# Preparation, attention and last stage of a fused attention and S4 kernel: narrow rows, no constant matmul ahead of the key burst, GpSimd work held back at unit borders

## The chip, the cores and the metric

One core of one Trainium2 chip. The time is device microseconds of one execution of the whole program. The profile is one execution, taken apart from the timed ones. All runs compared here are of the fast state, but for one of the 20 of e4, which is slow and left out of its ratio. The *granted clock* is the share of PE's full clock that the chip let through; in these traces it is 0.50 or 1.00 at any moment, and a mean for a stage or a run. A ratio is the mean time of one kernel's fast runs over the mean of the kernel before's fast runs of the same rounds, so it is not quite the ratio of the medians that stand beside it.

## The reference

Forward and backward of a gated mix of two blocks; thirteen outputs (the value and twelve gradients).

```python
B, S, D, H = 1, 2048, 576, 32             # head size 18; S4: L = 2048, N = 128 states
g = sigmoid((x * gate_w).sum(-1, keepdims=True))
a = attention(x, wqkv, wo)                # softmax(q k^T / sqrt(18)) v, then @ wo
b = S4(x, A, B, C, log_dt, Dskip)         # causal convolution with a kernel built from A, B, C
out = g * a + (1 - g) * b
_out, _vjp = jax.vjp(_f, ...)             # and the gradients for grad_out
```

## The kernel before

The attention works in 32 *units* (8 groups of 4 heads, times 4 query blocks of 512) of 32 *steps*. A step does two exponentials of 128x1024 on ScalarE: `PT` for the forward pass of one unit and `eb` (transposed scores) for the backward pass of the unit before. PE is fed in exactly the order below; all accumulators named accV, accQ, accK, accF share one PSUM bank, in turn. A *burst* is the run of matmuls into one of them, and its *eviction* is VectorE's reading it out. At a unit border VectorE makes `rl`, GpSimd from it `dOa`, and VectorE the sums `dl` from GpSimd's `prod`; between these GpSimd works through the *table products* of S4.

```python
NFILL = (0, 0, 1, 3)              # constant matmuls ahead of accV, accQ, accK bursts, and in accF
fill: mm(o_, lhsT=J_bf, rhs=fill_r)         # 128x128 times 128x512, a result nobody reads
for G in range(NTOT + OFF + 24):            # ... cut: what one step emits, in PE's order
    row(ps, KaT, QaT)                       # scores of the forward pass -> exp PT
    # G % 4 in (3, 0): accO += PT x Vtok
    row(ps, QaT, KaT)                       # transposed scores          -> exp eb
    row(ps, VaT, dOaT)                      # dP, then VectorE: ds = dP * PT
    # one of four: fill + accV, fill + accQ, fill + accK (key burst, 16 matmuls), accF (3 fills)
    # after accF: turn_ds, four PE transposes of a part of ds, in 7 of 8 cases
    ...                                     # evictions, products
    if G % NST not in (1, 2) or G >= NTOT:  # hold-back of GpSimd's table products
        e_emit(G)
```

A group's transposed keys are loaded as one block, and constants (zeros, ones, minus ones in the spare rows 18 to 31 of each head) are written on GpSimd's queue:

```python
nc.sync.dma_start(t_, KaT_d[g])             # 128 rows (4 heads x 32) of 4 KB
...
for t_ in rows:                             # Q, K, V
    nc.gpsimd.dma_start(t_[:, DH + 1:HP, sl], con[pt, 0:1, :].to_broadcast(...))
```

## Time and profile before

| | before |
|---|---|
| median, us (over all jobs 3161 to 3167) | 3162.5 |
| preparation, to the first forward exponential | 235.6 |
| attention, first PT to last eb exponential | 2119.3 |
| between attention and the weight gradients (mostly S4) | 603.8 |
| end, from the first weight-gradient matmul | 206.0 |

The stage marks are read off the timeline, and the same marks are used for every kernel below. The four rows sum to the profile's span of 3164.7. The prediction shows the profile's lines by stage.

### The profile page before, as it was taken

The numbers are of one execution on the slowest core, as the hardware profiler recorded it, in microseconds if no ns is written. First come the engines' busy times: TensorE is split into PE (matmuls) and PEld (weight loads), VectorE is DVE, ScalarE is ACT, GpSimd is POOL, SyncE is SP. The second block draws the span as 40 slices with busy tenths as digits, with TensorE's granted clock in tenths as the row PEclk, the third lists the DMA queues.
The fourth block names the chain that finished last, engine by engine and source line by source line (L and its number), as shares of the span: only waits on it lengthen the run. The fifth ranks groups of instructions, "written<-read, shape, count | busy, mean of one in ns | idle before, by whom it ended". The sixth has DMA issues, their size and how long they took to land. (4 is left out here: it accounts for less than half of the span.)

```text
span 3164.7 us, 70747 instructions
## 1 busy us (share of the span) xinstructions
PE 2580.8 (82%) x27165; PEld 1191.7 (38%) x27165; DVE 2460.3 (78%) x4533; ACT 2396.5 (76%) x2760; POOL 1811.8 (57%) x3387
## 2 busy tenths in 40 slices
PE   6668888888888888888888888888875787786668
PEld 2222222222233322323222322322224777776446
DVE  4244888888898888888888988888883888888634
ACT  3339999899899989999889988998845767675111
POOL 1009988988888898898898888888110000000010
PEclk9767999999899999999999988999986888888889
DMA  8865999888889988988998997897789778772895
GB/s 220 156 158 106 173 160 182 154 160 162 165 159 158 190 145 158 183 155 161 170 165 151 167 178 143 155 181 147 131 142 256 195 205 208 202 201 77 239 213 111
DMA packets 1411365, 533.55 MB, mean 169 GB/s; under 512 B 1309053, under 2 KB 1380190, under 8 KB 1401810
## 3 DMA queue, kind: packets, MB, share of 16 engines
q1 hardware_dynamic: 1380722, 463.03, 75.4%
q0 software_dynamic: 22416, 58.63, 7.5%
q10 hardware_dynamic: 7888, 7.38, 0.8%
q8 instruction: 212, 3.47, 0.4%
q14 instruction: 127, 1.04, 0.1%
HBM read 144.48 MB, written 102.83 MB: 78 GB/s over the span
## 5 line engine op out<-in xcount | busy, mean ns | idle before, releaser
L783 DVE TENSOR_TENSOR ds<-ps_P,PT 128x512 bf16<-128x512 f32 x2048 | 1316.0, 684 | 213.1 <-ACT eb L778 114.4
L773 ACT ACTIVATE PT<-ps_P 128x1024 bf16<-128x1024 f32 x1024 | 1049.5, 1027 | 164.8 <-PE ps_P L30 164.4
L778 ACT ACTIVATE eb<-ps_P 128x1024 bf16<-128x1024 f32 x1024 | 1051.8, 1027 | 32.3 <-PE ps_P L30 30.4
L552 POOL TENSOR_TENSOR et<-eG,eT 128x256 f32<-128x256 f32 x1152 | 701.0, 630 | 35.1
L30 PE MATMUL ps_P<-KaT_g,QaT_g 32*128 32x512 bf16 x2048 | 412.1, 393 | 86.7 <-ACT eb L778 86.5
L30 PE MATMUL ps_P<-dOaT,VaT_g 32*128 32x512 bf16 x2048 | 457.2, 394 | 5.9 <-DVE ds L783 4.4
L552 POOL TENSOR_TENSOR Eo<-et,et 128x256 bf16<-128x256 f32 x576 | 418.7, 727 | 43.1
L30 PE MATMUL ps_P<-QaT_g,KaT_g 32*128 32x512 bf16 x2048 | 416.5, 405 | 20.8 <-DMA Vtok_g<-VaT_d 12.6
L1074 POOL TENSOR_TENSOR SS<-m 128x96 f32<-128x96 f32 x18 | 7.9, 437 | 558.7 <-ACT m L1072 470.6
L30 PEld LDWEIGHTS <-QaT_g 32*128 32x128 bf16 x2048 | 154.4, 91 | 317.8 <-issue 316.6
L30 PE MATMUL accQ<-ds,Ktok_g 128*32 128x512 bf16 x2048 | 161.6, 391 | 105.5 <-DVE dvacc L489 67.1
L30 PE MATMUL accF<-ident_bf,J_bf 128*128 128x512 bf16 x783 | 233.8, 411 | 0.2 <-DVE dqa L504 0.2
L30 PEld LDWEIGHTS <-KaT_g 32*128 32x128 bf16 x2048 | 97.1, 91 | 341.1 <-issue 307.0
L30 PE MATMUL accO<-PT,Vtok_g 128*32 128x512 bf16 x2048 | 213.1, 402 | 0.0
L30 PEld LDWEIGHTS <-J_bf 128*128 128x128 bf16 x1103 | 91.7, 99 | 237.5 <-issue 207.4
L30 PE MATMUL accK<-dsT,Qtok_g 128*32 128x256 bf16 x4096 | 175.0, 296 | 0.0
L30 PE MATMUL accK<-ident_bf,J_bf 128*128 128x512 bf16 x256 | 103.0, 402 | 75.1 <-DVE dqa L509 59.9
L30 PE MATMUL accV<-eb,dOa 128*32 128x512 bf16 x2048 | 158.6, 387 | 2.2 <-DVE dsT L445 1.6
L930 ACT COPY E1e<-etp 128x1024 bf16<-128x1024 bf16 x144 | 135.9, 1043 | 17.8 <-PE etp L929 13.6
L30 PEld LDWEIGHTS <-Qtok_g 128*32 128x32 bf16 x4096 | 89.9, 100 | 157.8 <-issue 152.6
L30 PE MATMUL yp<-Rw,E1n 128*128 128x30 bf16 x1152 | 67.8, 232 | 87.9 <-DVE Rw L993 73.3
L30 PEld LDWEIGHTS <-E1n 128*128 128x128 bf16 x2304 | 96.7, 109 | 105.4 <-issue 104.9
(243 smaller groups left out, 3992.0 us busy)
## 6 DMA issues: line engine op xcount, KB each, us to landing
E_d<-Eo POOLq DMA_DIRECT2D x144, 256.0 KB, 3.6
E1n<-E_d SPq DMA_DIRECT2D x36, 1024.0 KB
xs<-xb_d SPq DMA_DIRECT2D x18, 1024.0 KB
T0w<-Kp_d SPq DMA_DIRECT2D x18, 1024.0 KB
Md_d<-mst SPq DMA_DIRECT2D x36, 288.0 KB
dsT<-ds SPq DMA_TRANSPOSE x512
dqkv_d<-dtk POOLq DMA_DIRECT2D x96, 72.0 KB, 3.8
skw<-Md_d SPq DMA_DIRECT2D x72, 64.0 KB
```

The costliest lines, as they stand in the source:

```text
L30: return nc.tensor.matmul(out, lhsT=lhsT, rhs=rhs, start=start, stop=stop, **kw)
L552: nc.gpsimd.tensor_tensor(out, a, b, op=op)
L773: nc.scalar.activation(U["PT"][i][:, j:j + 2, :], ps, ACT.Exp)
L778: nc.scalar.activation(e, ps, ACT.Exp)
L783: nc.vector.tensor_tensor(U["ds"][i][:, j, :], ps, U["PT"][i][:, j, :], op=A.mult)
L930: nc.scalar.copy(E_[:, 4 * q:4 * q + 4], pt_)
L1074: nc.gpsimd.tensor_tensor(o_[:, :, 0], m4[:, :, 0], m4[:, :, 3], op=A.subtract)
```

## The change

The intent: shorter constants and their stores out of the way of other transfers; a shorter loop at the key burst; no GpSimd work in the way at unit borders; fewer waits at the end. The core of the diff, cuts marked:

```diff
+    HS = DH + 2                                   # rows of K and V: 20 per head, not 32
-        QaT_d, KaT_d, VaT_d = ... [NG, P, S]
+        QKV_d = dram.tile([2 * HR + H * HP, S], BF, name="QKV_d")
...                                                # preparation
-            put_constants()                       # 20 stores on GpSimd's queue
+            for a_ in range(4):                   # 12 stores on SyncE's, before the first results
+                nc.sync.dma_start(rows[q_][:, y0:y1, sl], con[pt, q_:q_ + 1, :].to_broadcast(...))
+                xr_t = work.tile([P, TB, D], BF, tag="xr_t4", bufs=2, name="xr_t4")   # stores of four
...                                                # attention
-            NFILL = (0, 0, 1, 3)
+            NFILL = (0, 0, 0, 3)
+                def strip(k, g, c0, n):           # the next head's rows stand in as spare rows
+                    return bass.AP(tensor=QKV_d.tensor, ..., ap=[[WID[k] * S, 4], [S, HP], [1, n]])
-                    nc.sync.dma_start(t_, KaT_d[g])
+                    nc.sync.dma_start(t_, strip("K", g, 0, S))
-                    est = 0.07 + 2 * CE * n * 0.0023
+                    est = 0.21 + 2 * CE * n * 0.0018      # estimates that spread GpSimd's work
-                    for f in todo.pop(("f2", G), []):     # dl operations
-                        evs.append(f)
-                    for e_ in evs:
+                    for e_ in evs + todo.pop(("f2", G), []):
-                    if G % NST not in (1, 2) or G >= NTOT:
+                    if G % NST not in (0, 1, 2, NST - 1) or G >= NTOT:
...                                                # end
-                        nc.sync.dma_start_transpose(out=ob, in_=o_q)
+                            nc.tensor.transpose(pt_[:, c, :], o_q[:, c * P:(c + 1) * P], ident_bf)
-                nc.sync.dma_start(o12[d0:d0 + dsz, :], dgwb[0:dsz, c:c + 1])   # 576 single elements
+                nc.sync.dma_start(aps_out["out_12"]..., dgwb)                  # one row
+                    ob = work.tile([P, D], BF, tag="dwo_bf", bufs=3, name="dwo_bf")
```

## The prediction

> **What bounds the kernel now.** I read the busy time by stage first, then a steady stretch of the attention, the waits of each engine, and the queue of the preparation's transfers. By stage (columns: window, its length, busy us of PE, PE weight load, VectorE, ScalarE, GpSimd, the granted clock, the DMA share, GB/s):
>
> ```profile
> 0.00:233.50 233.50, 158.55 (x533) 60.15 (x533) 95.56 (x219) 71.61 (x121) 22.40 (x49) 0.79 0.79 179
> 277.60:2284.00 2006.40, 1733.01 (x17678) 591.49 (x17679) 1735.51 (x3068) 1844.04 (x1969) 1707.70 (x3182) 0.95 0.90 162
> ...
> 2944.70:3048.80 104.10, 65.18 (x332) 33.93 (x333) 43.99 (x66) 10.38 (x20) 12.03 (x19) 0.81 0.86 249
> 3048.80:3128.00 79.20, 79.15 (x635) 62.44 (x635) 51.49 (x95) 12.40 (x16) 0.00 (x0) 0.98 1.02 219
> ```
>
> The preparation (0 to 233.5, when the first score matmul starts) has no engine that is full: it is a chain of waits. The attention takes two thirds of the span and has four engines at 85 to 92%. The convolution (2371 to 2945) is untouched by the change and stays at 574. The end, 220 us, is PE work with three waits.
>
> A steady step of the attention, in order of start (start, duration, engine, line, operation; in brackets the idle time before it and who ended it):
>
> ```profile
> 758.71 0.68 DVE L509 SCALAR_TENSOR_TENSOR dqa<-accQ,dqa 128x512 f32<-128x512 f32 x1
> 759.44 0.38 PE L30 MATMUL accK<-ident_bf,J_bf 128*128 128x512 bf16 x1 [0.23 <-DVE dqa L509]
> ...
> 759.75 0.62 PE L30 MATMUL accK<-dsT,Qtok_g 128*32 128x256 bf16 x16
> ...
> 760.73 1.02 ACT L773 ACTIVATE PT<-ps_P 128x1024 bf16<-128x1024 f32 x1 [0.16 <-PE ps_P L30]
> ```
>
> The same ScalarE exponential stood at 753.11 one period before, so a period with one key burst is 7.62 us. It holds eight exponentials that start 0.92 apart when nothing is missing, 7.36 together. The missing 0.26 is a loop: the dqa eviction, the constant matmul into accK (0.31 from its start to the key burst's), the key burst of 16, the scores, the exponential. So here ScalarE and this loop are both bounds, ScalarE 0.26 behind.
>
> At a unit border (every 32 steps) more is lost:
>
> ```profile
> 787.07 0.26 DVE L397 RECIPROCAL rl<-accF 128x16 f32<-128x16 f32 x1 [0.32 <-PE accF L392]
> ...
> 792.06 0.45 DVE L410 TENSOR_REDUCE dl<-prod 128x16 f32<-128x288 f32 x1 [2.63 <-POOL prod L404]
> 792.63 0.68 DVE L489 TENSOR_TENSOR dvacc<-dvacc,accV 128x512 f32<-128x512 f32 x1
> ...
> 794.99 1.02 ACT L773 ACTIVATE PT<-ps_P 128x1024 bf16<-128x1024 f32 x1 [3.82 <-PE ps_P L30]
> ```
>
> GpSimd has table products in its queue when rl is ready, gets to dOa 3.5 us later, and VectorE, which works in order, stands 2.63 us at dl with the dvacc eviction behind it; PE and ScalarE then stand 3.5 and 3.8, and the granted clock is 0.50 for the next 6 us. The reciprocals rl, from 271.94 to 2292.16, are 31 units apart, 65.17 us each; 32 steps at the steady 7.62 per four would be 61.0. So a border costs 4.2 us on the mean, some none, some 7.
>
> GpSimd is the one to watch. Of its waits between 300 and 2200 only one is a wait for other engines, and its most frequent instruction is the table product:
>
> ```profile
> POOL dOa L402 <- DVE rl L397: 48.4, 14, 6.2
> ```
> ```profile
> L552 POOL TENSOR_TENSOR et<-eG,eT 128x256 f32<-128x256 f32 x1152 | 701.0, 630 | 35.1
> ```
>
> It is free only 48.4 of 1900 us. 1851.6 us over 1900/65.17 = 29.15 units are 63.5 us per unit: that is GpSimd's own pace, only 1.7 us under the present one.
>
> In the preparation, the in-order VectorE waits 28.8 us for the transposed d_a, and PE behind it 24.4 (in five waits 35.2) for the evictions that it owes. The transposes' own times show why:
>
> ```profile
> 72.02 22.64 SPq L243 DMA_TRANSPOSE d_aT<-d_a  x1
> 99.51 20.52 SPq L243 DMA_TRANSPOSE d_aT<-d_a  x1
> 183.92 4.36 SPq L243 DMA_TRANSPOSE d_aT<-d_a  x1
> 198.72 3.10 SPq L243 DMA_TRANSPOSE d_aT<-d_a  x1
> ```
>
> The same transfer takes 3 to 4 us when it is alone and 20 to 23 while GpSimd's queue stores 5.4 MB of constants (65 to 106 us). PE is idle from 88 to 112 and the granted clock is 0.50 from 80 to 120.
>
> At the end, two waits are aimed at:
>
> ```profile
> PE ps_a L30 <- DMA OT<-O_tok: 21.8, 1, 21.8
> PE ps_dwq L30 <- DMA dq_all<-dqkv_d: 16.5, 1, 16.5
> PE ps_dwo L30 <- ACT dwo_bf L1359: 8.6, 1, 8.6
> ```
>
> **What the Trainium skill says.** "TensorE: Matmul & The Clock Gate", Part 1: the clock is granted at 4/8 or 8/8 by how busy PE was in recent windows of about 3.4 us, and idle gaps above some 3 us should be avoided. The trace has only 0.50 and 1.00, in agreement, but at 782.9 it falls after 1.4 us of idle spread over 3.4, so the share counts and not only one long gap. "GPSIMD Engine Reference", 3.1: an operation with two input tensors takes about 2.6 cycles per element at 1.2 GHz, an estimate of 555 ns for 256 elements; the trace has 630, so such work has no slack to give. "DMA: Bandwidth & Descriptors", section on issuing engines not being separate queues: transfers issued by another engine share the same DMA engines. The trace agrees: GpSimd's stores slow SyncE's transposes from 3 to over 20 us. So moving the constants to SyncE does not make them cheaper; it only moves them in time. Same page, specifications: transfers below 512 B cost a read-modify-write. The small output of 576 two-byte pieces starts at 3129.00, and a store that starts 6 us after it took 15.32.
>
> **The change part by part.**
>
> *Preparation.* Constants and parameter blocks go out on SyncE's queue ahead of the first projection stores, with rows of 20 elements in place of 32 for K and V and fewer, larger blocks (12 for 30). They fall then before, not on, the d_a transposes. Gain: most of PE's 24.4 us stall, and the clock of the 40 us at 0.50: some 25 of these are busy after the stall is gone and could be run up to twice as fast, which I take as 10 us. The larger weight loads come after the first input transpose and x is loaded earlier: 7.2 + 2.7 of PE waits, I take 6. Larger stores (four tiles at once) and full 128-row operands: 3. Cost: the first projection store comes after 2.2 MB of constants, by my count of the queue at about 62 us and not 44; three staging buffers cover only part, so I charge 10 for a new stall, and 4 for the K strips that now load in four pieces. Sum: 24 + 10 + 6 + 3 + 9 - 14 = 38, where the 9 is the larger clock share in the dO part (176 to 222, where 0.83 and 0.66 are granted): less certain.
>
> *Attention, fill.* The constant matmul at the key burst goes (256 times). The loop falls from 7.62 to 7.31, below ScalarE's 7.36, so a period gains 0.26. There are 985 steps of 2.037 us here, about 246 periods, some 220 of them undisturbed: 57 us. In the tail, ten more periods, 3.
>
> *Attention, borders.* The products are held back in the last step of a unit and the first three, and the dl operations come behind the evictions. At 13 borders dl waited 27.5 us for prod; with the restart at half clock I put it at 1.5 times, 41.
>
> *The joint limit.* 57 + 41 = 98 us over 31 units would be 62.0 per unit, but GpSimd needs 63.5. Its work is not reduced, and the changed hold-back takes away places for it. So the two gains are worth together at most (65.17 - 63.5) x 31 = 52, and as no stage reaches its bound I take 0.8 of it: 42, plus 1 in the tail.
>
> *End.* Parameter gradients are turned by PE in place of six DMA transposes; but these 30 transposes stand in PE's order behind all 320 weight-gradient matmuls, so the work pool comes free nearly as late: 1. The O load waits for fewer transposes, 0 to 3. The small output becomes 32 wide matmuls and one row in place of 80 matmuls and 576 pieces, 16 x 0.15 = about 2. dwo_bf has three buffers: the 8.6 stall goes, and with it the cold run of the last 64 matmuls (10.1 against about 7.8): 11, less what the last store still takes. Sum about 11.
>
> Total: 38 + 43 + 11 = 92, from 3162.5 to 3070.
>
> **The rivals.** *(1) GpSimd is the bound at once, and unevenly:* where the held-back products pile up behind a border, every unit has slow steps, and the attention gains 15 to 20 only. For: the 63.5. Against: the new cost estimates spread its work more evenly over the units (it was up to 65.8 in some and 61.7 in others). Time 3095. *(2) The clock:* without the constant matmul PE's share falls from about 78 to 74% in the steady state; if that leaves a window under the threshold, matmuls double in time and the attention loses 50 to over 100. For: the fall at 782.9. Against: steady windows with 75% stand at 1.00, and the threshold seen lies near 58%. Time 3150 to 3250. *(3) The stall in the preparation only moves:* constants ahead of the first stores hold the staging buffers back for 15 to 20 us; gain there 10 to 20, time 3090. *(4) The preparation gains more:* with no idle gap PE stays warm through dO, 16 tiles of 3.43 us go toward 2: gain 55, time 3050. *(5) Less at the end:* the OT wait of 21.8 stays and the last store still ends the run: gain 5.
>
> **Range and chances.** The three parts are nearly independent: preparation 20 to 55, attention 20 to 57, end 5 to 25. Their spreads of about 15, 15 and 7 add in squares to 22; with a little for the clock the range is 3030 to 3112. The line of 2% is at 3100, 1.3 such spreads above 3070. So faster by over 2% has 0.80, within 2% 0.17, slower 0.03, for rival 2.
>
> **What would show it.** Right: the group accK from the constant is gone; a steady period is 7.36 to 7.5; the wait of dl for prod is below 10 in all; dOa's wait for rl shrinks from 48.4 toward 0 and units are about 63.5 apart (GpSimd the bound). The first score matmul is at about 195, the d_a transposes take 3 to 6 us each, and PE shows a new wait for staging buffers between 48 and 64. The dwo wait is gone and the OT wait is still near 20; the convolution is 574. Wrong: a granted clock in the attention below 0.93; units still 65 apart with dOa waiting (then the loop was not the bound); units under 63 (then GpSimd's pace was not one); a first score matmul after 215 or before 180.

## The result

3162.78 us median (3155.69 to 3165.82, 4 runs) against 3163.26; ratio 0.9997, interval 0.9979 to 1.0016. The time is the same. The stages are not:

| us, from the profiles | before | after | difference |
|---|---|---|---|
| preparation | 235.6 | 206.6 | -29.0 |
| attention | 2119.3 | 2153.8 | +34.5 |
| to the first weight-gradient matmul | 603.8 | 602.0 | -1.8 |
| end | 206.0 | 199.1 | -6.9 |
| span | 3164.7 | 3161.5 | -3.2 |

So two parts gained 36 us as meant, and the attention, where 43 were expected, lost 34. Stages of the kernel after (same columns as in the prediction):

```profile
0.00:204.50 204.50, 127.44 (x532) 69.90 (x532) 94.90 (x220) 70.00 (x120) 11.21 (x29) 0.84 0.79 189
...
243.00:2300.00 2057.00, 1759.86 (x17522) 599.38 (x17521) 1745.92 (x3087) 1860.41 (x1978) 1716.50 (x3196) 0.92 0.92 159
```

The granted clock of the attention is 0.92, where it was 0.95. That is the first trace of what happened.

**The steady step.** The group of the constant matmul at accK is gone, and yet the period is 7.62 us, as before. Kernel after, one period, in order of start:

```profile
961.48 0.62 PE L30 MATMUL accK<-dsT,Qtok_g 128*32 128x256 bf16 x16 [0.23 <-DVE dqa L523]
961.58 1.03 ACT L790 ACTIVATE eb<-ps_P 128x1024 bf16<-128x1024 f32 x1
...
962.67 0.39 PE L30 MATMUL ps_P<-dOaT,VaT_g 32*128 32x512 bf16 x2
...
963.12 1.29 DVE L795 TENSOR_TENSOR ds<-ps_P,PT 128x512 bf16<-128x512 f32 x2 [0.16 <-PE ps_P L30]
...
963.88 0.38 PE L458 MATMUL dst_p<-ident_bf,ds 128*128 128x128 bf16 x4
...
964.20 0.39 PE L30 MATMUL ps_P<-QaT_g,KaT_g 32*128 32x512 bf16 x2
...
964.63 1.02 ACT L785 ACTIVATE PT<-ps_P 128x1024 bf16<-128x1024 f32 x1 [0.18 <-PE ps_P L30]
```

The gap of ScalarE is no longer behind the key burst; it stands one step later, behind the four transposes of ds. The chain: `eb` must end, PE can then do the scores with dO (962.67), VectorE the first product ds (963.12), PE the transposes (963.88), which stand in PE's order *ahead* of the next scores (964.20), and those feed the exponential at 964.63. From `eb` to that `PT` it is 3.05 us, and three exponentials need only 3 x 0.92 = 2.76. The same chain is in the kernel before:

```profile
759.54 1.03 ACT L778 ACTIVATE eb<-ps_P 128x1024 bf16<-128x1024 f32 x1
...
761.84 0.38 PE L444 MATMUL dst_p<-ident_bf,ds 128*128 128x128 bf16 x4
...
762.59 1.02 ACT L773 ACTIVATE PT<-ps_P 128x1024 bf16<-128x1024 f32 x1
```

Again 3.05 us from `eb` (759.54) to `PT` (762.59). But the page gave this exponential no wait: the one before it had been delayed by the constant matmul, so ScalarE was not free before 762.57 (the eb at 761.65 and 0.92). The second loop left only some 0.02 us to gain, and the first one hid it.

**The borders.** VectorE's wait for prod is nearly gone, and GpSimd's for rl has grown (waits of the kernel after, 300 to 2200; total, times, longest):

```profile
DVE dl L424 <- POOL prod L418: 4.1, 2, 3.0
```
```profile
POOL dOa L416 <- DVE rl L411: 87.0, 24, 7.5
```

So GpSimd was not the bound: it waits 87 us here against 48. Units are 66.3 us apart (243.0 to 2298.3, 31 of them) where they were 65.17. By step within the unit, against the steady step: the first eight steps cost 3.04 us per unit, not 3.90; the other twenty-four cost 2.28, not 0.21. Two thirds of these 2.28 (8 units of 5.76 us in 30) stand in every fourth unit, where the load of a group's keys is followed, 7 to 12 us later, by stalls that cost 4.6 to 8.5 us.

**The key load.** DMA share (tenths) in 40 slices of the 17 us from the load on; after, then before:

```profile
DMA  7379324999932313231222222243999990099999
```
```profile
DMA  8699995949998990000899999903999999599259
```

After: for some 17 slices, 7 us, the engines stand at 0.1 to 0.4, and 58 to 116 GB/s flow. I read this as one transfer working on about a quarter of the engines. Before, the same 512 KB left the engines busy with other work. Behind the load stand the DMA transposes of ds; VectorE's product ds waits for them (300 to 2200; no such wait is listed before):

```profile
DVE ds L795 <- DMA dsT<-ds: 26.0, 9, 6.7
```

**The clock.** In long stretches of the attention the granted clock is 0.50 although PE never stops (kernel after, unit 16; PE busy is the second number):

```profile
1243.50:1247.00 3.50, 3.50 (x30) 0.66 (x30) 1.88 (x3) 2.89 (x3) 3.27 (x6) 0.50 0.77 114
1247.00:1250.50 3.50, 3.48 (x32) 0.94 (x33) 3.37 (x6) 2.96 (x3) 3.02 (x6) 0.50 0.25 81
1250.50:1254.00 3.50, 3.44 (x19) 1.06 (x16) 1.84 (x4) 2.18 (x3) 3.26 (x6) 0.50 0.92 181
...
1261.00:1264.50 3.50, 3.44 (x19) 1.02 (x16) 1.77 (x4) 2.25 (x3) 3.33 (x6) 0.50 1.26 155
1264.50:1268.00 3.50, 3.50 (x30) 0.70 (x30) 1.97 (x4) 2.82 (x4) 3.04 (x6) 0.50 1.25 170
```

A period takes 10.4 us there, not 7.62 (exponentials at 1250.6 and 1261.0). I counted such stretches in the clock record of each trace, from the start of unit 1 to the end of unit 30. Their lengths are multiples of 3.41 us:

| kernel | constant matmul | stretches | of 1 / 2 / 3 or more windows | longest, us | in all, us |
|---|---|---|---|---|---|
| before | yes | 35 | 21 / 12 / 2 | 17.1 | 181 |
| after | no | 35 | 14 / 8 / 13 | 30.7 | 293 |

As many stretches, but longer: 112 us more at half clock. At (10.4 - 7.62) / 10.4 = 0.27 us lost per us this is an estimate of 30 us (a fit of time against the recorded clock of each run gives 0.16 to 0.30 in the kernels timed 20 times or more). It may not be added to what the experiments below take apart, since a stall can itself be followed by half clock: putting the constant matmul back gives 6 us in the changed kernel (e1, within noise) and 13 with the key strip mended (e11 against e12).

**Preparation and end.** The stall of 24 us is gone, a new one has come. Waits of PE up to 235, and two of SyncE's issues:

```profile
PE ps L30 <- DVE sq L227: 21.1, 8, 5.5
PE psr L30 <- ACT xr_t L191: 18.1, 6, 16.5
```
```profile
52.27 10.19 SPq L172 DMA_DIRECT2D QKV_d<-con  x12
62.50 0.43 SPq L173 DMA_DIRECT2D zero_d<-con  x1
63.04 0.85 SPq L193 DMA_DIRECT2D xr_d<-xr_t  x2
...
79.68 8.00 SPq L254 DMA_TRANSPOSE d_aT<-d_a  x1
...
92.40 10.96 SPq L254 DMA_TRANSPOSE d_aT<-d_a  x1
```

The store that frees the xr_t buffers stands behind the twelve constants and goes out at 63.04; PE stands from 49.9 to 66.4. The later transposes hold SyncE's queue for 8 and 11 us in place of 20 and more. At the end the chain of waits now ends in PE work alone:

```profile
3134.13 4.01 PE pgw L30 x32
3138.14 19.84 PE ps_dwo L30 x160
```

The 8.6 us wait and the cold run are gone, and the OT wait is 9.0, not 21.8; but the new transposes and their own waits now stand in that time, and from the last weight-gradient matmul to the first output matmul it is 19.1 us where it was 22.2. Against this the small output's matmuls take 4.0 us at once, and from the first output matmul to them the loop takes 87.5 us where it took 83, at a clock of 0.93.

### The profile page after: what moved, and what is told of

It is laid out like the page before. It is cut to its first block, busy times and chain, and to the rows that moved or that the text cites. A ratio compares the mean times of both kernels' runs of the same rounds, so it can differ in the third digit from the quotient of the medians.

```text
span 3161.5 us, 70115 instructions
## 1 busy us (share of the span) xinstructions
PE 2566.7 (81%) x26891; PEld 1209.8 (38%) x26891; DVE 2461.5 (78%) x4531; ACT 2405.2 (76%) x2765; POOL 1801.6 (57%) x3371
## 3 DMA queue, kind: packets, MB, share of 16 engines
q14 instruction: 127, 1.04, 0.1%
## 5 line engine op out<-in xcount | busy, mean ns | idle before, releaser
L30 PE MATMUL ps_P<-KaT_g,QaT_g 32*128 32x512 bf16 x2048 | 420.6, 401 | 125.8 <-ACT eb L790 125.0
L30 PE MATMUL ps_P<-dOaT,VaT_g 32*128 32x512 bf16 x2048 | 491.5, 403 | 33.0 <-DVE ds L795 25.1
L30 PE MATMUL ps_P<-QaT_g,KaT_g 32*128 32x512 bf16 x2048 | 425.8, 414 | 22.2 <-DMA Vtok_g<-QKV_d 14.1
L30 PE MATMUL accF<-ident_bf,J_bf 128*128 128x512 bf16 x783 | 240.6, 420 | 0.2 <-DVE dqa L518 0.2
L30 PE MATMUL accO<-PT,Vtok_g 128*32 128x512 bf16 x2048 | 222.0, 420 | 0.0
L30 PEld LDWEIGHTS <-Qtok_g 128*32 128x32 bf16 x4096 | 114.9, 99 | 181.4 <-issue 177.7
L30 PE MATMUL accV<-eb,dOa 128*32 128x512 bf16 x2048 | 168.2, 407 | 2.1 <-DVE dsT L459 1.8
L30 PEld LDWEIGHTS <-J_bf 128*128 128x128 bf16 x847 | 67.6, 101 | 190.5 <-issue 161.4
L523 DVE SCALAR_TENSOR_TENSOR dqa<-accQ,dqa 128x512 f32<-128x512 f32 x192 | 130.4, 679 | 0.0
```

Source lines behind the costliest of these rows:

```text
L30: return nc.tensor.matmul(out, lhsT=lhsT, rhs=rhs, start=start, stop=stop, **kw)
L523: nc.vector.scalar_tensor_tensor(o_, acc, c_scale, a_, op0=A.mult, op1=A.add)
```

## The experiments

Theory A: a second loop of the same length holds the steady period. Theory G, formed after the first runs: the constant matmul's worth was the clock, and without it every stall costs more. Rivals: B, the constant matmul was the bound and its gain was lost elsewhere; C, the hold-back moves the loss; D, an engine holds the period. "Attention" is from the profile of each run, the ratio is to the kernel before (after: 0.9997).

**e1: the constant matmul back.**

```diff
-            NFILL = (0, 0, 0, 3)
+            NFILL = (0, 0, 1, 3)
```

> The changed kernel with the one constant matmul at the key burst put back, nothing else. Theory A (a second loop, as long as the one through the constant matmul, holds the period: exponential, score with dO, VectorE's product ds, the transposes of ds on PE, and behind them in PE's order the next scores): the steady period of four steps stays 7.62 us and the time stays within 10 us of the changed kernel, near 3163. Rival B (the constant matmul was the bound, as I predicted, and its 57 us were gained but lost again elsewhere): the period goes from below 7.5 to 7.62 and the time rises by 40 to 60 us, to 3205 to 3220.

3157.01 us (20 runs), 0.9985; period 7.62. Theory A holds: at the key burst it gains nothing to leave the matmul out. B is out. The attention of this run's profile is 2153.9, as in the changed kernel, so alone the matmul does not bring the loss back.

**e2: the key strip in four transfers.**

```diff
-                    nc.sync.dma_start(t_, strip("K", g, 0, S))
+                    for j in range(4):
+                        r0 = ROW0["K"] + (4 * g + j) * WID["K"]
+                        nc.sync.dma_start(t_[HP * j:HP * (j + 1), :], QKV_d[r0:r0 + HP, :])
```

> The changed kernel with each load of a group's key strip (128 rows of 4 KB, now one transfer whose slowest dimension is the 4 heads) given out as four transfers of 32 rows each. Theory A (the one transfer runs on a quarter of the DMA engines, takes some 12 us, and holds up the transposes of ds behind it once per group of four units): the stalls of 4 to 8 us in the middle of every fourth unit go, and the time falls by 25 to 45 us, to some 3120 to 3138. Rival C (the slow middle of units comes from GpSimd's held-back products that bunch up behind the border): the time stays within 10 us of 3163.

3140.95 us, 0.9938: 22 us less than the changed kernel, a little under what I gave. DMA share from the load on, 17 us:

```profile
DMA  9223999879994999999989939905999999999493
```

The quarter-full stretch is gone. Steps 8 to 31 of every fourth unit lost 5.76 us in the changed kernel and lose 2.44 here, and the wait for the transposes has fallen from 26.0 us:

```profile
DVE ds L797 <- DMA dsT<-ds: 6.4, 5, 3.3
```

The edit changes two things, the slowest dimension and the number of transfers; e5 bears on which of them counts.

**e3: the transposes of ds behind the next scores.**

```diff
-                            evs.append(turn_ds(UN[(g, b)], q_))
+                            at(("turn", G + 1), lambda U=UN[(g, b)], q_=q_: turn_ds(U, q_)())
...                    # after the scores of PT in the next step:
+                    for f in todo.pop(("turn", G), []):
+                        f()
```

> The changed kernel with the four PE transposes of ds put behind the next step's first score matmuls instead of ahead of them, nothing else. Theory A (these transposes are the loop that holds the steady period at 7.62): the period falls to 7.36 to 7.45, ScalarE's own pace, and the time falls by 20 to 50 us, less the more GpSimd's pace of 63.5 us per unit binds. Rival D (VectorE or GpSimd holds the period): 7.62 stays and the time stays within 10 us of 3163.

3124.14 us, 0.9887; period 7.50, not 7.36 to 7.45. Theory A holds, D is out as it was put: with the same work on every engine, the order alone gives 38 us. But 7.50 shows a third loop (see e8).

**e4: the border as before** (hold-back of two steps, dl operations ahead of the evictions).

```diff
+                    for f in todo.pop(("f2", G), []):       # ahead of the bursts' evictions
+                        evs.append(f)
-                    for e_ in evs + todo.pop(("f2", G), []):
+                    for e_ in evs:
-                    if G % NST not in (0, 1, 2, NST - 1) or G >= NTOT:
+                    if G % NST not in (1, 2) or G >= NTOT:
```

> The changed kernel with both parts of the border change undone: products held back only in two steps of a unit as before, and the dl operations ahead of the step's evictions as before. Theory A (the border change gained about 26 us in the first eight steps of the units; the rest of the loss is the strip): the time rises by 15 to 35 us, to 3180 to 3200, and the waits of dl for prod come back toward 27 us. Rival C (the hold-back only moves the products into later steps, and costs there what it gains): within 10 us of 3163, with the slow steps in the middle of units fewer.

3144.29 us (20 runs, 3122.59 to 3178.07, the highest of them slow), 0.9952, interval 0.9934 to 0.997. My expectation was wrong: undoing the border change gains 18 us by the medians, where I had read a gain of 26 out of the first eight steps of the units. The spread is wide, and this run's profile (3158.7) is above its median. Nor do the waits of dl for prod come back toward 27 us: they are 8.6.

**e5: rows of 32 per head again, constants where the change put them.**

```diff
-    HS = DH + 2
+    HS = HP
-                    return bass.AP(tensor=QKV_d.tensor, ..., ap=[[WID[k] * S, 4], [S, HP], [1, n]])
+                    return QKV_d[r0:r0 + P, c0:c0 + n]
```

> The changed kernel with rows of K and V again 32 per head in memory, so that every strip is one contiguous block of 128 rows; the constants grow again (K's and V's 14 spare rows hold -1 and 1, which meet only zeros or unused rows), still stored by SyncE ahead of the first projection stores. Theory A (the narrow strips, read as four pieces, cost the attention some 35 us, of which giving the key strip out in four got back 19): from the first to the last exponential the time falls from 2154 to 2115 to 2130 us, near the 2119 of the kernel before, with no mid-unit stalls; the preparation gets longer by 5 to 20 us for 3 MB more of constants. Total 3130 to 3150. Rival E (the strip costs only what the four-way split recovered): the attention stays above 2135.

3149.62 us, 0.9944; attention 2136.5, preparation 219.2 to the first exponential. The preparation is 12.6 us longer, as expected; the attention is not back at 2119 and is about what e2 gives (2139.5). So the layout costs the attention about what the four-way split gets back (rival E), and another cause is left. Here the strip is again one transfer, but of 128 rows, and the quarter-full stretch is gone too (17 us from 533, the load at 533.5); VectorE's wait for the transposes of ds is 2.9 us. So one transfer alone does not make the stretch; what e2 and e5 share is that no load of the strip has a slowest dimension of 4.

```profile
DMA  9999989989109999999988915799999999969577
```

**e6: only the hold-back as before.**

```diff
-                    if G % NST not in (0, 1, 2, NST - 1) or G >= NTOT:
+                    if G % NST not in (1, 2) or G >= NTOT:
```

> The changed kernel with the products held back in two steps of a unit as before, the dl operations left behind the evictions. Undoing both parts gave about 14 to 18 us. If the longer hold-back is what costs (GpSimd stands idle at a border, 87 us in all against 48, and catches up behind it), this alone gives 10 to 20, to 3143 to 3153. If the late dl operations cost (the dO transpose behind them starts later and PE waits for it), this gives under 5, and the other half gives it.

3145.63 us (5 runs, 3129.93 to 3172.01), 0.9944, interval 0.9903 to 0.9986. The hold-back seemed to be the part that costs; see e10 and e12. VectorE's wait for prod is 2.9 us here too, so the hold-back was not what removed it. Nor is it the late dl operations alone: with early ones e8 has 27.4 but e4 only 8.6, and e14, with late ones, has 35.3. What removed it is not settled.

**e7: e3 with the constant matmul back** (the edits of e1 and e3).

> The changed kernel with the transposes of ds behind the next scores, as in the run that gave 3124, and the constant matmul at the key burst put back. Theory A (two loops of the same 7.62 us side by side, each enough to hold the period): the period returns from 7.50 to 7.58 to 7.62 and the time rises to 3140 to 3160, so that each of the two edits alone gives nothing or little where the other loop stands. Rival F (only the transposes' loop counted, the constant matmul never did): 7.50 stays and the time is within 8 us of 3124.

3147.43 us, 0.9940; period 7.60. Two loops side by side: with the transposes moved, the constant matmul costs 0.10 us per period, and 23 us in all. Without that move it cost nothing.

**e8: transposes late, key strip in four, border as before** (the edits of e2, e3 and e4).

> The changed kernel with all three repairs: transposes of ds behind the next scores, the key strip in four transfers, the border as before. If the gains of 38, 21 and 14 to 18 add up: 3085 to 3095. GpSimd's pace of 63.5 us per unit allows about 2018 us from the first to the last unit border, against 2055 in the changed kernel, so I expect it to take part of the sum: 3095 to 3115.

3110.16 us, 0.9821. As expected, the parts do not add up fully. What holds its 7.50 is, by the trace, the next loop of the same kind; of its lines:

```profile
1220.25 0.68 DVE L505 TENSOR_TENSOR dvacc<-dvacc,accV 128x512 f32<-128x512 f32 x1
...
1220.98 0.62 PE L30 MATMUL accQ<-ds,Ktok_g 128*32 128x512 bf16 x8 [0.22 <-DVE dvacc L505]
...
1221.53 0.39 PE L30 MATMUL ps_P<-QaT_g,KaT_g 32*128 32x512 bf16 x2
...
1221.96 1.02 ACT L791 ACTIVATE PT<-ps_P 128x1024 bf16<-128x1024 f32 x1
```

The query burst waits for an eviction, and the next scores stand behind the burst: the two exponentials start 1.13 us apart, the others 0.90 to 0.92.

**e9: the kernel before with only the constant matmul taken away.**

```diff
-            NFILL = (0, 0, 1, 3)
+            NFILL = (0, 0, 0, 3)
```

> The kernel before with only the constant matmul at the key burst taken away. Theory G (the constant matmul's worth is the clock: it fills the array, and without it the granted clock stays at 0.50 longer after each stall): the steady period stays 7.62; the stretches at 0.50 between units 1 and 30, of which 33 of 35 lasted one or two windows of 3.4 us in the kernel before (181 us in all), get a tail of three to nine windows (220 to 300 us in all), and the time rises by 5 to 35 us above the kernel before. Rival H (the longer cold stretches of the changed kernel come from its stalls alone): stretches as before and the time within 5 us of the kernel before.

3170.48 us (20 runs, 3151.92 to 3187.81) against 3161.47; 1.0024, interval 1.0007 to 1.004. The edit that I had put at -57 us makes the kernel 9 us slower. The period stays 7.62. Theory G holds. The time alone would leave rival H standing (2 to 13 us by the interval); the clock does not: 11 stretches of three windows or more against 2 (table below), and a mean clock of 0.896 over its 20 runs against 0.906 over 46 of the kernel before.

**e10: the kernel before with only the longer hold-back.**

```diff
-                    if G % NST not in (1, 2) or G >= NTOT:
+                    if G % NST not in (0, 1, 2, NST - 1) or G >= NTOT:
```

> The kernel before with only the longer hold-back of the products (four steps of a unit in place of two). Undoing it in the changed kernel gave some 15 us. If the hold-back costs by itself: 10 to 20 us above the kernel before. Theory G (what it costs in the changed kernel is the longer cold stretches that follow its stalls, which the constant matmul would have ended): within 8 us of the kernel before, and the wait of dl for prod falls from 27 us to under 10.

3161.47 us (20 runs), 0.9998: nothing. The wait of dl for prod does not fall (31.1 us), against what I had expected.

**e11: the changed kernel with key strip in four, old hold-back, constant matmul back (the edits of e1, e2 and e6); e12: the same without the constant matmul (e2 and e6).**

> The changed kernel with the constant matmul back, the old hold-back and the key strip in four transfers, so that of the change only the preparation, the last stage, the late dl operations and the new estimates of GpSimd's work are left. If the three parts account for all of the attention's loss of 34 us, the attention is back at 2110 to 2125 us and the gains of the preparation (29) and the end (7) show: 3120 to 3135. If it stays above 3140, some part of the loss is still open.

> As the run before it, but without the constant matmul. Theory G: cold stretches longer than there, 5 to 25 us more time, 3125 to 3155, and a wider spread between runs. Rival B (taking the constant matmul away is a gain once the stalls are mended): 10 us or more faster than that run.

e11: 3128.59 us, 0.9907, attention 2119.9. e12: 3141.90 us (11 runs, 3133.06 to 3158.39), 0.9938. This closes the sum by medians: changed kernel 3162.8; key strip in four, 3141.0 (-21.8); also the old hold-back, 3141.9 (+0.9); also the constant matmul, 3128.6 (-13.3). Together 34.2, the whole loss of the attention. By the ratios, which take out the difference between jobs, the steps are 19, 0 and 10, together 28, where each ratio is known to 5 to 9 us either way; and the last depends on the order, as e1 shows. The loss is made up for rather than undone place by place: in e11 the first eight steps of a unit still cost 3.2 us, not 3.9, and the others 1.0, not 0.2, most of it in every fourth unit (3.2 us against 0.7 before; one profile each), so some of the key load's cost stays. With the strip mended the hold-back costs nothing; its 17 us in e6 (wide interval) and the 18 of both parts in e4 stand only beside the unmended strip, and why is not settled.

**e13: all bursts late too, with the constant matmul; e14: the same without; e15: only the transposes late, with it.** All three have the edits of e2, e3 and e6, and e13 and e15 that of e1; e13 and e14 also put the bursts behind the next step's first scores:

```diff
-                        ACC.append(accB(("accV", "accQ", "accK")[ph]))
-                        fill(ACC[0], NFILL[ph])
+                        def begin(ph=ph):
+                            ACC.append(accB(("accV", "accQ", "accK")[ph]))
+                            fill(ACC[0], NFILL[ph])
+                        at(("turn", G + 1), begin)
-                            evs.append(dq_burst(g, b, q_))
+                            at(("turn", G + 1), lambda g=g, b=b, q_=q_: dq_burst(g, b, q_)())
...                    # dv_burst and the key burst in the same way
```

> The changed kernel with old hold-back and key strip in four, and on PE the transposes and all three bursts put behind the next step's first scores, the constant matmul back in front of the key burst. Theory A+G (loops through PE's order set the period, the constant matmul shortens cold stretches): with every loop opened the constant matmul costs ScalarE nothing, the period is 7.36 to 7.42 and cold stretches are mostly one or two windows: 3075 to 3100. If GpSimd's pace of 63.3 us per unit binds instead: 3100 to 3112, its wait for rl near 20.

> The same without the constant matmul. Theory G: the period is the same, 7.36 to 7.42, as the constant matmul is no longer in a loop; the cold stretches are longer, and the time is 0 to 15 us above the run with it. If the constant matmul still costs: below it by 5 or more.

> Only the transposes late, the constant matmul back, old hold-back, late dl operations, key strip in four. The run with 7.50 and no constant matmul gave 3110; here the loop through the constant matmul gives 7.60, some 20 us more in the steady state, and shorter cold stretches give back 10: 3110 to 3125.

e13: 3131.91 us, 0.9886, period 7.82. e14: **3098.64 us, 0.9783**, interval 0.9758 to 0.9808, period 7.50: the fastest of all, some 2.2% faster than the kernel before, though the interval leaves open whether it is over 2%. e15: 3121.94 us, 0.9860, period 7.60. My expectation for e13 failed: the matmul costs 0.32 us per period there. I take it to be out of the old loop and in a new one, since the accumulators share one bank and everything behind the burst moves with it; no run tests this apart. The period of 7.36 was reached by none. In e14 the wait that held e8 is gone, and yet 7.50 stays: the exponentials are now late at two other places, behind the accF matmuls and, one later, behind the transposes of ds (1.02 and 1.04 us apart, not 0.90). e14 gains 11 us on e8 at the same period (it also has the late dl operations), with fewer stretches at half clock; it stays open why it needs no constant matmul for short ones.

| kernel | constant matmul | stretches at 0.50 | 1 / 2 / 3 or more | longest, us | in all, us |
|---|---|---|---|---|---|
| e1 | yes | 41 | 21 / 10 / 10 | 17.1 | 256 |
| e3 | no | 30 | 12 / 8 / 10 | 17.1 | 222 |
| e7 | yes | 34 | 14 / 18 / 2 | 17.1 | 201 |
| e9 | no | 34 | 20 / 3 / 11 | 30.7 | 232 |
| e10 | yes | 32 | 19 / 11 / 2 | 10.2 | 160 |
| e11 | yes | 35 | 25 / 6 / 4 | 13.7 | 171 |
| e12 | no | 38 | 18 / 9 / 11 | 34.1 | 324 |
| e13 | yes | 29 | 25 / 3 / 1 | 13.7 | 120 |
| e14 | no | 25 | 13 / 10 / 2 | 10.2 | 133 |
| e15 | yes | 40 | 28 / 10 / 2 | 10.2 | 184 |

Five pairs differ only in the constant matmul: before and e9, e1 and after, e7 and e3, e11 and e12, e13 and e14. In each the total is lower with it; each is one profiled execution, but the mean clocks of all timed runs agree: 0.906 with it and 0.896 without, 0.902 and 0.892, 0.905 and 0.898, 0.908 and 0.892, 0.920 and 0.913. The other kernels without it (e2, e4, e5, e6, e8) have 9 or 10 stretches of three windows or more; e1, with it, has 10 too, so with the unmended strip it does not make them rare. In time the pairs do not agree: without it the kernel is 9, 6 (within noise) and 13 us slower in the first, second and fourth, and 23 and 33 us faster in the third and fifth, where the matmul stands in a loop that holds the period.

## Why the prediction was wrong

**Step "Attention, fill"** failed, and it was the largest. "The loop falls from 7.62 to 7.31, below ScalarE's 7.36, so a period gains 0.26" took the loop whose wait the profile named for the only one. The chain through the transposes was 0.02 us shorter. It had no wait line of its own because ScalarE was hardly free when it arrived. The term of 57 us (60 with the tail) was nothing at the steady period, and by e9 it is -9 us in the time. ScalarE's own pace was also misread a little: where nothing holds them, as in e14, the exponentials start 0.90 apart, not 0.92.

**Rival 2, the clock,** had the right part and the wrong mechanism. I tested the share of busy time in the *steady* state, and there the clock does stay at 1.00. What the constant matmul did was to shorten the cold stretches *after a stall* (little of it in e1, with the unmended strip). I weighed the clock by busy time ("the threshold seen lies near 58%", which is the share of one window, from 779.5 to 782.9, ahead of one fall); in the stretches above PE is 98 to 100% busy and the clock stays at 0.50. So busy time as the profile gives it is not what decides. That a constant matmul counts for more because it is 128*128 in the trace, where the scores are 32*128 and the bursts 128*32, is a conjecture; no run tells it apart. Two of my own signs of failure came true: a clock below 0.93 (0.92), and units no closer than 65 with dOa waiting (66.3, and 87 us).

**Step "the K strips that now load in four pieces",** charged with 4 us once, in the preparation's sum, was mis-sized: the load comes once per group, the transposes of ds behind it come late, and it costs 22 us (e2).

**Step "borders"** (41 us) failed: the wait of dl for prod fell from 26.5 to 4.1 between 300 and 2200, as said, but the time did not follow. The hold-back alone is worth nothing in the kernel before (e10), and undoing both parts in the changed kernel leaves the wait at 8.6 and makes it 18 us faster (e4; 14 by the ratios). So taking that wait's length as time to be gained was the error; what takes its place is not settled.

**Step "the joint limit"** (63.5 us per unit on GpSimd) was not reached: no kernel's attention comes under 2084.8 us, and GpSimd still waits 25 us for rl in e14, whose units of 64.0 us come near it. No run puts it to the test. It did no harm only because the gain that it was to cut was not there.

**Preparation** was right in kind: 29 against 38. The new stall was foreseen "between 48 and 64" and charged with 10; it is 16.5, and its buffer is xr_t, not the projection's staging. The first score matmul is at 204.5, inside my limits of 180 and 215. (The 20 to 23 us read as a transposing transfer's time are the times for which SyncE's queue was held by it.) **The end** gained 6.9 against 11: the dwo part is as said, but the small output costs 4.0 us of PE in one piece and the loop is 4.7 us longer. That the OT wait stays near 20 did not come true (9.0), but the new transposes and their waits fill most of the difference.

## What to carry to other kernels

When a wait is to be removed, time every chain into the same consumer, not only the one that the profile names: a second chain shows no idle time as long as the first delays the consumer past it, and here the slack was 0.02 us. A matmul with a useless result can be worth its time through the clock after stalls (9 and 13 us here), and can cost more than that where it stands in the loop that holds the period (23 and 33 us); look at how long the stretches at half clock last, not only at the mean clock of a stage. Here a load whose slowest dimension was 4 left the DMA engines at 0.1 to 0.4 for 7 us and delayed what was queued behind it; with a slowest dimension of 32 the kernel was 22 us faster. Look at the order of a load's dimensions when a layout changes.

## What the Trainium skill lacked or had wrong

- "TensorE: Matmul & The Clock Gate", Part 1, says that the clock is warm after one busy window of about 3.4 us. The window length agrees (all stretches are multiples of 3.41 us), the condition doesn't as it is put: here, in a stretch of 30.7 us at 0.50, PE was 98 to 100% busy by the profile in each 3.5 us from 1243.5 to 1268, seven such windows (a matmul's end is modelled there, but a period of 10.4 us in place of 7.62 agrees with the half clock), and one 128x128x512 constant matmul per period changed how long such stretches last. The page does not say what counts as busy.
- "DMA: Bandwidth & Descriptors", section on why a DMA increments its semaphore by 16, says that the number of DMA engines is the largest number up to 16 that divides both sides' slowest dimensions. The trace agrees: with a slowest dimension of 4 the DMA share stood at 0.1 to 0.4 for 7 us, and four transfers of 32 rows took 22 us off the time. What the page does not go into is what such a load costs the transfers queued behind it: VectorE's wait for the transposes of ds was 26.0 us with it, 6.4 with the four transfers and 2.9 with one of 128 rows.
